# Memsets of the first batch's value tiles, written ahead of the loads into the same tiles

## The chip, the cores and the metric

The kernel runs on one core of a Trainium2 chip. The metric is the device time of one execution in microseconds (us), taken as the median of several executions. The profile is that of one execution; its times count from the start of its span.

## The reference

The reference is an attention with a relative position bias, followed by a feed-forward layer with a "snake" activation. Cut to what is computed:

```python
# q, k, v: [8 batches, 8 heads, 576 rows, 64]; bias_table: [32 buckets, 8 heads]
scores = (1 / sqrt(64)) * q @ k.transpose(0, 1, 3, 2)
bucket = ...            # of abs(row - column), 32 buckets
scores = scores + bias_table[bucket].transpose(2, 0, 1)[None]
attn = softmax(scores, axis=-1)
x = (attn @ v)  -> rows [8 * 576, 8 * 64]
h = x @ w_in                                   # [4608, 2048]
g = h + sin(alpha * h) ** 2 / (alpha + 1e-9)
out = g @ w_out                                # [4608, 512], float32
```

## The kernel before

The work is done batch by batch, eight times attention and then the feed-forward layer on blocks of 512 rows. In attention, keys and queries lie transposed (tiles `kT`, `qT`), one score tile of 128 keys by 512 queries for two heads is made by two matmuls, ScalarE (ACT) takes its exponential into `u`, VectorE (DVE) multiplies the stretch near the diagonal by a table of exponentiated biases (`m`, and its shifted copy `mh`), and TensorE (PE) multiplies with the values in `v`. The last 64 of the 576 keys go through tiles of their own, `kt` and `vh`. Each head has 65 columns in the value tiles: 64 of values and one column of ones, whose product is the sum of the softmax.

There are two tiles of each kind, for even and odd batches. Batch 0 is loaded straight from the inputs. Head pair 0 of its keys and queries arrives in `natx` through the queues of SP and ACT (L463), is cast by DVE (`cast0`, L498, and L542) and ACT (L543), is transposed by PE (L572) and copied to `kT` and `qT` by DVE (L561). Head pairs 1 to 3 arrive in `nat` through POOL's queue (L463) and are transposed by L578. The values come through POOL's queue too, four loads of 128 rows (L445, tile `v`) and two of the last 64 rows (L457, tile `vh`); a load writes columns 0 to 63 of each head, and a memset (L485) the column of ones. POOL then issues the loads of `w_in` (L468), of batch 1's keys and queries, of `w_out` (L472) and of batch 1's values.

Before any of this, PE runs matmuls on a tile of zeros (`zz`), and DVE clears `zz` (L528), `vh` and `v` (`clear_v`, L481 to L485), `kt` (`clear_k`, L477 and L478), makes `less_last` (a difference of unit vectors for the bias table) and clears the second pair of value tiles.

The order of the instructions is fixed when the program is built. The head of the program, which the diff touches, runs in the order in which its lines stand. Behind it a planner (`Plan`) orders the work of all engines by priorities and estimated times; each engine executes its own list in order. Which waits an instruction carries follows from the order of the source: whoever comes second into a tile waits for who came first. This holds for the tile as a whole here: the memset of the column of ones and the loads of the other 64 columns write different addresses, and still the later one waits for the earlier one. `STATIC` holds four loads that are issued in the head: keys and queries of head pair 1, and the first two of the value loads. The other two value loads and the two of `vh` are issued by the planner's first tasks on POOL.

```python
STATIC = ((1, (1, 0)), (1, (1, 1)), (0, (0,)), (0, (1,)))
LOADS = ((0, (2,)), (0, (3,)), (0, (4,)), (0, (5,)), (1, (2, 0)), ...
```

Of the kernel before, what the change touches and what calls it, by code (L numbers as in the profile page):

```python
# [303 lines left out]
def kernel(  # L304
# [11 lines left out]
    nc = tc.nc  # L316
# [44 lines left out]
    zz = sgl.tile([128, 512], F16, name="zz")  # L361
# [93 lines left out]
    def load_vt(t, z):  # L455
        vq = v[t].rearrange("(hp two) s d -> two s hp d", two=2)
        nc.gpsimd.dma_start(  # L457
            out=vhs[t % 2][64 * z : 64 * z + 64, :, VC * z : VC * z + D], in_=vq[z, 512:S]
        )
# [16 lines left out]
    def clear_k(eng, i):  # L476
        eng.memset(kts[i][0:64, :, 64:128], 0.0)  # L477
        eng.memset(kts[i][64:128, :, 0:64], 0.0)  # L478

    def clear_v(eng, i):  # L480
        eng.memset(vhs[i][0:64, :, VC : 2 * VC], 0.0)  # L481
        eng.memset(vhs[i][64:128, :, 0:VC], 0.0)
        eng.memset(vhs[i][0:64, :, D : D + 1], 1.0)
        eng.memset(vhs[i][64:128, :, VC + D : VC + D + 1], 1.0)
        eng.memset(vs[i][:, :, :, D : D + 1], 1.0)  # L485
# [34 lines left out]
    def load_v0(c):  # L520
        if c < 4:
            load_v16c(0, c)
        else:
            load_vt(0, c - 4)

    for t, f in STATIC:
        (load_kq1 if t else load_v0)(*f)
    nc.vector.memset(zz, 0.0)  # L528
    clear_v(nc.vector, 0)
    clear_k(nc.vector, 0)  # L530
    clear_k(nc.vector, 1)
    nc.vector.tensor_scalar(
# [773 lines left out]
```

## Time and profile before

| what | value |
|---|---|
| median of 3 executions | 381.05 us (380.95 to 381.33) |
| the profiled execution, its own time | 381.91 us |
| its span, first to last instruction | 380.2 us |
| mean granted clock of TensorE | 0.987 |
| PE busy | 365.0 us, 96% of the span |
| ACT busy | 313.5 us, 82% |
| DVE busy | 267.4 us, 70% |
| POOL busy | 87.8 us, 23% |

A row of the timeline gives the start of a group of instructions, its busy time, the engine, the line, the operation, the tile written and the tile read, the count (x), and in brackets the idle time of the engine just before and what ended it. PEld is the loading of weights into TensorE. A row of the windows gives each engine's busy time in a stretch, with the count in brackets, then the granted clock (PEclk, 1.00 is full), the time that the DMA engines were busy in it, and GB/s. A row of the DMA issues ends with the median time from the issue to the landing of the data.

### The profile page before, as it was taken

What the parts mean: (1) busy time and instruction counts of PE and PEld (TensorE: products, weight loads), DVE (VectorE), ACT (ScalarE), POOL (GpSimd) and SP (SyncE); (2) the same over time, 40 slices, a digit from 0 to 9 for tenths busy, and PEclk for the clock granted to TensorE, in tenths of its full rate; (3) what the DMA queues carried; (4) which work ended last, traced back from release to release, by engine and by line L of the source; (5) the groups of instructions that cost most, each with busy time, mean ns of one, the idle gap of its engine ahead of it and who ended that gap; (6) DMA issues with size and microseconds to landing.
All of it is one profiled execution on the core that took longest, in us unless ns stands there. A gap on an engine that the chain in (4) does not pass through costs nothing.

```text
span 380.2 us, 9067 instructions
## 1 busy us (share of the span) xinstructions
PE 365.0 (96%) x3662; PEld 199.9 (53%) x3662; DVE 267.4 (70%) x585; ACT 313.5 (82%) x428; POOL 87.8 (23%) x111
## 2 busy tenths in 40 slices
PE   3688999999999999999999999999999999999996
PEld 1556445554456445686464445544567455444443
DVE  0799698759775886678777967696769676879200
ACT  1199799979998999889997999798979997989211
POOL 4584250009100270019000900082006000000000
PEclk9599999999999999999999999999999999999999
DMA  9599999269921899289925992499339322000122
GB/s 135 39 164 209 203 154 118 57 126 94 157 78 47 132 133 156 58 133 109 165 73 93 132 162 65 106 117 157 88 73 154 55 66 53 9 1 30 57 81 83
DMA packets 147993, 39.16 MB, mean 103 GB/s; under 512 B 136416, under 2 KB 142960, under 8 KB 147952
## 3 DMA queue, kind: packets, MB, share of 16 engines
q0 software_dynamic: 99664, 18.06, 59.6%
q1 hardware_dynamic: 47920, 20.11, 22.7%
q8 instruction: 28, 0.46, 0.5%
q10 hardware_dynamic: 368, 0.43, 0.4%
q14 instruction: 13, 0.11, 0.1%
HBM read 36.84 MB, written 16.52 MB: 140 GB/s over the span
## 4 chain that ended last, share of the span: by engine, by line
PE 87%; DMA 6%; DVE 3%; POOL 2%; issue 1%; ACT 0%; ACTq 0%; DVEq 0%; POOLq 0%
PE pb L488 86%; DMA w_out<-in_moe_w_out_dram 5%; DMA v<-in_v_dram 1%; POOL nat L463 1%; PE pb L578 1%; PE pb L1089 0%; DVE kT L561 0%; DVE g L1147 0%; PE pb L572 0%; DVE kt L601 0%; POOL v L445 0%; POOL kt L601 0%; DVE tmp_a L713 0%; DVE m L561 0%; ACT s L1133 0%
## 5 line engine op out<-in xcount | busy, mean ns | idle before, releaser
L771 ACT ACTIVATE u<-pb 128x1024 f16<-128x1024 f32 (+1 forms) x146 | 136.9, 1019 | 12.1 <-PE pb L488 11.3
L488 PE MATMUL pb<-w_out,g 128*128 128x512 f16 (+2 forms) x592 | 138.9, 374 | 0.7 <-DMA w_out<-in_moe_w_out_dram 0.7
L488 PE MATMUL pb<-xT,w_in 128*128 128x512 f16 (+4 forms) x704 | 127.3, 340 | 0.0
L1133 ACT ACTIVATE s<-pb,alphaT 128x512 f16<-128x512 f32 x144 | 92.5, 693 | 15.0 <-PE pb L488 14.5
L1147 DVE SCALAR_TENSOR_TENSOR g<-sq,inv_a,pb 128x512 f16<-128x512 f16 x144 | 100.7, 743 | 4.9 <-ACT sq L1140 3.1
L488 PEld LDWEIGHTS <-w_in 128*128 128x128 f16 x704 | 64.8, 98 | 58.9 <-issue 1.0
L488 PEld LDWEIGHTS <-g 128*128 128x128 f16 x592 | 53.4, 98 | 60.9 <-issue 6.7
L803 DVE TENSOR_TENSOR u<-u,m 128x768 f16<-128x768 f16 (+1 forms) x128 | 62.0, 492 | 32.0 <-ACT u L771 30.1
L488 PEld LDWEIGHTS <-u 128*128 128x128 f16 x1152 | 44.1, 97 | 9.7 <-issue 3.5
L1140 ACT ACTIVATE sq<-s 128x512 f16<-128x512 f16 x73 | 45.7, 640 | 2.0 <-DVE g L1147 1.2
L441 POOL COPY kt<-kT 64x256 f16<-64x256 f16 x12 | 5.0, 421 | 174.4 <-DMA kT<-staged_k 174.1
L488 PE MATMUL pb<-v,u 128*128 128x65 f16 x1024 | 44.3, 193 | 0.1
L488 PE MATMUL pb<-qT,kT 64*128 64x64 f16 (+1 forms) x512 | 42.1, 287 | 1.6 <-ACT u L771 1.4
L1142 DVE TENSOR_TENSOR sq<-s 128x512 f16<-128x512 f16 x71 | 29.6, 421 | 16.5 <-ACT s L1133 16.0
L445 POOL DMA_DIRECT2D v<-in_v_dram x32 | 28.4, 898 | 12.9 <-DVE v L485 4.2
L1018 DVE TENSOR_TENSOR xn<-pb,rd 128x256 f16<-128x256 f32 (+2 forms) x59 | 28.5, 483 | 2.0
L488 PE MATMUL pb<-vh,u 128*128 128x130 f16 x128 | 28.2, 220 | 0.0
L488 PEld LDWEIGHTS <-kT 64*128 64x128 f16 x512 | 16.5, 94 | 21.7 <-issue 14.4
L561 DVE COPY outs<-pb 128x512 f32<-128x512 f32 x29 | 19.9, 686 | 2.1 <-PE pb L488 1.9
L559 ACT ACTIVATE outs<-pb 128x512 f32<-128x512 f32 (+2 forms) x8 | 4.4, 544 | 19.8 <-PE pb L488 19.8
L1211 ACT ACT_TABLE_LOAD x15 | 19.2, 1283 | 0.3
L1017 DVE RECIPROCAL rd<-pb 128x4 f32<-128x4 f32 (+2 forms) x59 | 10.9, 185 | 11.4 <-PE pb L488 11.4
(72 smaller groups left out, 190.7 us busy)
## 6 DMA issues: line engine op xcount, KB each, us to landing
out_dram<-outs SPq DMA_DIRECT2D x35, 256.0 KB, 2.3
v<-in_v_dram POOLq DMA_DIRECT2D x32, 128.0 KB, 4.6
staged_k<-in_k_dram POOLq DMA_DIRECT2D x6, 576.0 KB, 9.0
staged_q<-in_q_dram POOLq DMA_DIRECT2D x6, 576.0 KB, 12.1
w_out<-in_moe_w_out_dram POOLq DMA_DIRECT2D x4, 512.0 KB, 21.4
w_in<-in_moe_w_in_dram POOLq DMA_DIRECT2D x2, 512.0 KB, 8.7
w_in<-in_moe_w_in_dram POOLq DMA_DIRECT2D x1, 1024.0 KB, 13.8
xT<-xn SPq DMA_TRANSPOSE x47, 2.6
```

What stands on the lines that cost most here:

```text
L445: nc.gpsimd.dma_start(out=vs[t % 2][:, c, :, 0:D], in_=vp[128 * c : 128 * c + 128],)
L488: nc.tensor.matmul(out=out, lhsT=lhsT, rhs=rhs, start=start, stop=stop)
L561: k_of(e).tensor_copy(out=o, in_=i)
L771: nc.scalar.activation(out=o, in_=x, func=AF.Exp, scale=0.125)
L803: nc.vector.tensor_tensor(out=io, in0=io, in1=m2[:, 2 * p : 2 * p + 2, x0 : x0 + hi - lo], op=ALU.mult)
L1017: nc.vector.reciprocal(out=r, in_=x[:, :, :, D])
L1018: nc.vector.tensor_tensor(out=xn[:, 0:n].rearrange("p c (z d) -> p c z d", z=2), in0=x[:, :, :, 0:D], in1=r.unsqueeze(3).to_broadcast([128 ...
L1133: nc.scalar.activation(out=s16.v, in_=h.v, func=AF.Sin, scale=alphaT[:, f : f + 1])
L1140: nc.scalar.activation(out=sq.v, in_=s16.v, func=AF.Square)
L1142: k_of(e).tensor_tensor(out=sq.v, in0=s16.v, in1=s16.v, op=ALU.mult)
L1147: nc.vector.scalar_tensor_tensor(out=gcell[b].v[:, f, :], in0=sq.v, scalar=inv_a[:, f : f + 1], in1=h.v, op0=ALU.mult, op1=ALU.add,)
L1211: nc.scalar.preload_act_table_set(name)
```

## The change

The two lines that clear `zz` and the value tiles of even batches move from behind the four loads of `STATIC` to ahead of them. Nothing else changes.

```diff
+    nc.vector.memset(zz, 0.0)
+    clear_v(nc.vector, 0)
     for t, f in STATIC:
         (load_kq1 if t else load_v0)(*f)
-    nc.vector.memset(zz, 0.0)
-    clear_v(nc.vector, 0)
     clear_k(nc.vector, 0)
     clear_k(nc.vector, 1)
```

The memsets are on DVE and the loads on POOL, so neither engine's list changes its order; what changes is who waits. On DVE, at the very start of the program, the difference is this (`v_72` and `vh_74` are the value tiles of even batches, `kt_70` the key tile; DMASW4 and DMASW3 count the landings of the first two value loads; minus is before, plus is the change):

```order
-L528 MEMSET zz 128x256
+L526 MEMSET zz 128x256
 L481 MEMSET vh_74 64x4x65
 L482 MEMSET vh_74 64x4x65
 L483 MEMSET vh_74 64x4
 L484 MEMSET vh_74 64x4
-L485 MEMSET v_72 128x32 [waits DMASW4_49,DMASW3_49]
+L485 MEMSET v_72 128x32
 L477 MEMSET kt_70 64x4x32
 L478 MEMSET kt_70 64x4x32
```

The memset of the column of ones loses its wait for two loads; the rows around it are as they were. On POOL, in the head of the program behind the loads of head pair 1, the difference is this (`nat_96` holds head pairs 1 to 3; the wait is for a memset on DVE):

```order
 L463 DMA nat_96<-in_k_dram 96x2x384
 L463 DMA nat_96<-in_q_dram 96x2x384
-L445 DMA v_72<-in_v_dram 128x8x64 x2
 L445 DMA v_72<-in_v_dram 128x8x64 [waits DVE_49]
-L445 DMA v_72<-in_v_dram 128x8x64
+L445 DMA v_72<-in_v_dram 128x8x64 x3
 L457 DMA vh_74<-in_v_dram 64x4x64
 L457 DMA vh_74<-in_v_dram 64x4x64 [waits DMASW0_49]
```

The wait for DVE moves from the third value load to the first. PE, ACT and SP have the same rows and the same waits as before.

## The prediction

> **What bounds the kernel now.** I read the chain of work that ended last first, since it tells which stretch of the span could give anything back.
>
> ```profile
> 4.13 0.89 POOL v L445
> 5.02 4.44 DMA v<-in_v_dram
> ...
> 11.81 0.59 DVE natx L498
> ...
> 26.07 18.92 DMA w_out<-in_moe_w_out_dram
> ...
> 45.03 3.83 PE pb L488 x17
> ```
>
> The chain enters the value load in the first 10 us, comes out on DVE, and goes by POOL's queue into the landing of `w_out`; from 45 us on it is on PE almost without a break until 377. So a shift of the first 45 us passes through to the end unchanged, as long as the later stretches hang on nothing but PE's own list. The page's row of PE, busy tenths in 40 slices of 9.5 us, says the same:
>
> ```profile
> PE   3688999999999999999999999999999999999996
> ```
>
> From the fifth slice to the last but one it stands at 9; only the first four have anything to give.
>
> Next the timeline of DVE in the head.
>
> ```profile
> 2.01 0.06 DVE L484 MEMSET vh<- 64x4 f16 x1
> 9.71 0.09 DVE L485 MEMSET v<- 128x32 f16 x1 [7.63 <-DMA v<-in_v_dram]
> 10.60 0.38 DVE L532 TENSOR_SCALAR less_last<-idf_sb 32x128 f32<-32x128 f32 x1
> 11.81 0.58 DVE L498 CAST natx<-natx 96x768 f16<-96x768 f32 x1
> 12.30 0.39 DVE L542 CAST natx<-natx 96x384 f16<-96x384 f32 x1
> 13.14 0.76 DVE L561 COPY kT<-pb 128x576 f16<-128x576 f16 x1 [0.45 <-PE pb L572]
> 14.57 0.76 DVE L561 COPY qT<-pb 128x576 f16<-128x576 f16 x1 [0.19 <-PE pb L572]
> 18.18 1.22 DVE L561 CAST m<-pb 128x1024 f16<-128x1024 f32 x1 [0.31 <-PE pb L488]
> ```
>
> DVE stands still for 7.63 us ahead of one memset of 0.09 us, and everything of batch 0 is queued behind it: the cast of the first keys starts at 11.81.
>
> **The wait that goes.** Without it L485 follows L484 (its end is 2.07, and some 0.05 passes between neighbours) at 2.12 instead of 9.71, so DVE's list behind it is 7.59 us earlier, if nothing else is late. `less_last` would come at 3.01; its input is made by POOL in the row at 2.66 below and is ready at 2.86. The cast L498 would come at 11.81 - 7.59 = 4.22. What is late next are its data.
>
> ```profile
> natx<-in_k_dram ACTq DMA_DIRECT2D x1, 144.0 KB, 3.4
> ...
> 0.80 0.43 ACTq L463 DMA_DIRECT2D natx<-in_k_dram  x1
> 2.66 0.20 POOL L509 CAST idf_sb<-id_sb 32x32 f32<-32x32 f16 x1
> 5.19 0.52 ACT L543 ACTIVATE natx<-natx 96x384 f16<-96x384 f32 x1 [1.69 <-DMA natx<-in_q_dram]
> ```
>
> The keys of pair 0 land at 0.80 + 3.4 = 4.2, so L498 keeps about its 7.55. The queries land at 5.19, where ACT's row shows who waited for them; L542 can't start before, so it gains 12.30 - 5.19 = 7.1, and a new wait of about 0.4 us stands ahead of it. The copy to `kT` then starts at 5.6 (L542's end), a gain of 7.5. **First term: 7.5 us.**
>
> **The clock.** The second effect is on PE.
>
> ```profile
> 1.26 3.70 PE L488 MATMUL pb<-zz 128*128 128x512 f16 x12 [1.26 <-DVE zz L528]
> 12.44 0.66 PE L572 MATMUL pb<-id_sb,natx 96*128 96x96 f16 x6 [7.48 <-DVE natx L498]
> 15.21 0.69 PE L578 MATMUL pb<-id_sb,nat 96*64 96x96 f16 x12
> 17.00 0.61 PE L488 MATMUL pb<-qT,kT 64*128 64x512 f16 x2
> 19.61 0.39 PE L488 MATMUL pb<-qT,kT 64*128 64x512 f16 x2
> 21.83 0.45 PE L578 MATMUL pb<-id_sb,nat 96*64 96x96 f16 x12
> ...
> 8.75:9.00 0.25, 0.00 (x0) 0.00 (x0) 0.00 (x0) 0.00 (x0) 0.00 (x0) 0.96 0.10 6
> 9.00:9.50 0.50, 0.00 (x0) 0.00 (x0) 0.00 (x0) 0.00 (x0) 0.00 (x0) 0.50 0.00 0
> 19.00:19.25 0.25, 0.25 (x2) 0.00 (x0) 0.25 (x1) 0.25 (x1) 0.11 (x1) 0.56 0.85 92
> ```
>
> PE ends its first matmuls at 4.96 and sits idle until 12.44; the granted clock falls to 0.50 near 8.97, four microseconds into the gap, and comes back near 19.2. In between the same two score matmuls take 0.61 instead of 0.39, and twelve transposes 0.69 instead of 0.45. With the wait gone PE has its next transposes at 4.22 + 0.59 + 0.05 = 4.9, right behind its first matmuls, and the idle stretch that cost the clock isn't there. I take the clock as staying at 1.00. What that is worth on the path is not PE's halved time but DVE's idle time behind PE: 0.45, 0.19 and 0.31 us in the rows above, and 0.29, 0.34 and 0.40 between them, 2.0 us together. Bounds are 0 (the clock falls all the same) and 2.0 less the 0.45 that the new wait of L542 has taken, about 1.5. The transposes shrink by a third (0.69 to 0.45), which in DVE's idle time is about 0.25 us at each of the three later copies, and some 0.45 of the 0.6 at the bias table's small matmuls: I take 1.2. DVE and ACT then run ahead by 7.5 + 1.2 = 8.7 at 18 us, and ACT is dense from there to 36.9, so PE would ask for `w_out` 8.7 earlier. **Second term: 1.2 us, on DVE, ACT and PE.**
>
> The Trainium skill (page "TensorE: Matmul & The Clock Gate", part 1, on the clock gate) states that the clock halves after an idle window of about 3.4 us and returns after about 3.4 us of sustained work. The fall here after 4.0 us of idle agrees; the return after 6.8 us of nearly full work does not. By that rule the second term would stand in full, since no gap of 3.4 us is left.
>
> **POOL and the loads.** The chain goes by `w_out`, so POOL's list decides what can be kept.
>
> ```profile
> 4.12 1.80 POOL L445 DMA_DIRECT2D v<-in_v_dram  x2
> 10.09 1.76 POOL L445 DMA_DIRECT2D v<-in_v_dram  x2 [4.16 <-DVE v L485]
> 11.81 1.34 POOL L457 DMA_DIRECT2D vh<-in_v_dram  x2
> 16.77 0.51 POOL L601 COPY kt<-kT 64x64 f16<-64x64 f16 x2 [3.61 <-DVE kT L561]
> 17.22 0.65 POOL L463 DMA_DIRECT2D nat<-in_k_dram  x1
> 19.69 0.83 POOL L648 COPY mh<-m 64x768 f16<-64x768 f16 x1 [0.58 <-ACT m L559]
> 21.08 2.26 POOL L468 DMA_DIRECT2D w_in<-in_moe_w_in_dram  x3
> ```
>
> The added wait of the first value load is for a memset that is over by about 2.2, and POOL gets there at 4.12: it costs nothing, and the cover is 1.9 us. The third value load needn't wait any more (4.16 us), so POOL issues all six in one go: 4.12 + 1.80 + 1.76 + 1.34 = 9.02. The copy L601 waits for DVE's second `kT`, which ends at about 8.5 with the clock kept, so POOL goes on at once: 0.45 for the copy, then three loads of `nat` (17.22 to 19.11, 1.9 us) to 11.4. ACT's part of `m` is done by then (before: 0.58 us of waiting), so `mh` starts at 11.4 instead of 19.69, 8.3 earlier, and `w_in` at about 12.8, 8.2 earlier. `w_out` is three issues and one copy later on the same list.
>
> The DMA engines must follow. They are drained at 8.75 now, and the last two value loads and `vh` then move at leisure:
>
> ```profile
> 12.00:14.00 2.00, 1.56 (x13) 1.34 (x14) 1.45 (x4) 0.02 (x1) 1.16 (x2) 0.50 1.53 98
> 14.00:16.00 2.00, 2.00 (x43) 1.85 (x42) 1.26 (x5) 0.16 (x1) 0.00 (x0) 0.50 0.95 60
> 35.00:40.00 5.00, 4.98 (x59) 3.10 (x58) 2.87 (x10) 3.96 (x7) 1.40 (x2) 1.00 1.30 201
> ```
>
> That is 1.53 + 0.95, with the edges 2.6 us of engine time; put right behind the first two loads it lasts to about 11.4, before `w_in` starts. `w_in`, batch 1's keys and queries and `w_out` then stream at some 200 GB/s as now (last row), so the landing of `w_out` moves by the 8.2 of its issue, less perhaps 0.1 for the tail of the value loads. **What is kept: 8.1 us.** PE, 8.7 early, finds `w_out` only 8.1 early, and its wait there grows:
>
> ```profile
> 45.03 0.38 PE L488 MATMUL pb<-w_out,g 128*128 128x512 f16 x1 [0.74 <-DMA w_out<-in_moe_w_out_dram]
> ```
>
> from 0.74 to about 1.3 us. Bounds from both sides: 7.5 if the clock brings nothing, 9.0 if the loads keep up fully and the 0.74 is partly given back.
>
> **The sum.** The profiled execution took 381.91 (span 380.2 and 1.71 around it), 0.86 above the median. 381.91 - 8.1 = 373.8 for such an execution, and 0.86 less for the median: **372.9 us**.
>
> **Rivals.**
>
> *The clock falls all the same.* For it: between 12.44 and 19.2 PE was busy nearly throughout and the clock stayed low, so transposes and small matmuls may not count as full work. Against: the fall needed four idle microseconds. All of the head then moves by the first term only: 381.05 - 7.5 = 373.5.
>
> *DVE's work holds up POOL.* DVE is now busy between 2.1 and 9, where POOL issues eight loads that it issued beside an idle DVE. If each DVE instruction that reads and writes SBUF shut POOL out for its time (`less_last` 0.38, L498 0.58, L542 0.39, copies of `kt` 0.35, together 1.7), `w_out` would keep 8.1 - 1.7 = 6.4: 374.6. Against it: the value loads at 10.09, beside memsets and `less_last`, took 1.76, and those at 4.12, beside an idle DVE, 1.80; and `vh` at 11.81, beside both casts, took 0.67 each. The Trainium skill (page "SBUF — State Buffer", section "Who interferes with whom") states this as an exclusive lock of a port pair that VectorE's fast modes and GpSimd share, with the loser fully blocked. The issues just named show nothing of that size.
>
> *More than forecast.* If the stream of loads catches up, PE keeps 8.7 to 9.0: 372.2.
>
> *The wait is only moved.* Were DVE's memset late, POOL's first value load would wait for it; that needs a delay of over 1.9 us, and would leave 381 as it is.
>
> *Slower: POOL's queue waits for a value load.* Each load on POOL's queue waits for the one eight places ahead, so the first load of `w_in` waits for the third value load. That one is now issued at 5.9 into a busy queue, no longer at 10.1 into an empty one. The landing times of the value loads range widely:
>
> ```profile
> DMA to landing us min/median/max: 3.7/9.7/22.2
> ```
>
> If it took the longest, 22.2 us, it would land at 28.1, `w_in` would start 7.0 later than the 21.08 of now, and with it `w_out`: 388. It is slower than before from a landing at about 21, 15 us after the issue. Against it: that maximum comes from the stretch in which `w_in` and `w_out` fill the queue, and the second of the two early loads landed 4.44 us after its issue at 5.02 (the chain's row), with the engines as full as they will be for the third.
>
> **How the numbers follow.** Forecast, 372.9 (372.3 to 373.2): 0.52. Clock falls, 373.5: 0.24. POOL held up, 374.6: 0.09. More, 372.2: 0.11. Wait only moved, 381: 0.01. Slower: 0.02; the last 0.01 is for a gain of less than 6 us by other causes. The range reaches from the better case with 0.4 us for the uncertain sizes to the held-up POOL: 371.8 to 374.7. What a measurement of this kernel can tell from no change is about 0.2%, 0.8 us: faster 0.97, same 0.01, slower 0.02.
>
> **What the profile afterwards would show.** L485 at about 2.1 with no idle time; L498 at 4.2 to 4.3; L542 at 5.2 behind a short wait for the queries; the granted clock at 1.00 throughout (or a fall between 8 and 12, in which case the second term goes); all six value loads issued by 9.1; `w_in` at about 12.8; PE's first matmul with `w_out` at about 36.9, behind a wait of 1 to 1.5 us; and the rest of the timeline the same but for that shift. The prediction is wrong if the wait of PE for `w_out` is far longer, or if the stretch after it no longer runs at PE's pace.

## The result, and the profile after

| | before | changed |
|---|---|---|
| median, 4 executions each | 381.19 us (380.95 to 381.43) | 375.25 us (374.40 to 375.51) |
| ratio | 1 | 0.984 (0.9823 to 0.9858) |
| the profiled execution | 381.91 us | 375.07 us |
| its span | 380.2 us | 373.4 us |

The change makes the kernel 5.9 us faster. 8.1 were forecast, and the range ended at 374.7.

The page of the changed kernel, busy tenths and granted clock in slices of 9.3 us:

```profile
PE   8799999999999999999999999999999999999996
PEclk9789999999999999999999999999999999999999
```

Of the four slices that had something to give, the first goes from 3 to 8 and the last two reach 9, but the second only goes from 6 to 7. The clock, forecast at full, dips in the second and third.

The timeline of DVE in the changed kernel (start, busy time, engine, line, operation):

```profile
2.23 0.09 DVE L485 MEMSET v<- 128x32 f16 x1 [0.16 <-issue]
4.34 0.58 DVE L498 CAST natx<-natx 96x768 f16<-96x768 f32 x1
5.18 0.37 DVE L542 CAST natx<-natx 96x384 f16<-96x384 f32 x1 [0.26 <-DMA natx<-in_q_dram]
9.17 1.23 DVE L561 CAST m<-pb 128x1024 f16<-128x1024 f32 x1
```

The wait of 7.63 us is gone, a new one of 0.26 stands ahead of L542, and the cast to `m` comes at 9.17 instead of 18.18, 9.0 earlier. The head of the program did what the first two terms said.

The timeline of PE in the changed kernel:

```profile
12.50 0.39 PE L488 MATMUL pb<-qT,kT 64*128 64x512 f16 x2 [0.37 <-ACT u L771]
14.27 0.69 PE L578 MATMUL pb<-id_sb,nat 96*64 96x96 f16 x12 [1.38 <-DMA nat<-in_k_dram]
17.02 0.61 PE L488 MATMUL pb<-qT,kT 64*128 64x512 f16 x2
38.26 0.38 PE L488 MATMUL pb<-w_out,g 128*128 128x512 f16 x1 [0.46 <-DMA w_out<-in_moe_w_out_dram]
```

At 12.89 PE has nothing left: the keys of head pair 2 have not landed, and it waits 1.38 us for them. Then the slow durations are back, 0.69 for twelve transposes and 0.61 for two score matmuls. The first matmul with `w_out` starts at 38.26; 36.9 was forecast. Three windows of the same kernel show the clock around that wait (columns: the stretch, its length, PE, PEld, DVE, ACT, POOL, granted clock, mean share of the DMA engines, GB/s; the share is no time, as the text ahead of the prediction calls it, and can pass 1: before, 12 to 13 us shows 1.82, 13 to 14 shows 1.24, and the window over both 1.53):

```profile
13.00:14.00 1.00, 0.00 (x0) 0.00 (x0) 0.69 (x3) 0.95 (x1) 0.85 (x2) 1.00 0.99 115
14.00:20.00 6.00, 5.73 (x62) 2.62 (x62) 4.35 (x8) 4.27 (x5) 5.56 (x9) 0.52 1.04 142
20.00:38.00 18.00, 16.91 (x211) 10.68 (x210) 14.23 (x41) 16.34 (x26) 6.49 (x9) 0.97 1.23 206
```

From 14 to 20 us the clock is at half, PE is nearly full, and DVE and ACT stand still for over a quarter of the time. The lead of 9.0 us that the head had won shrinks here. The chain of work that ended last, in the changed kernel:

```profile
4.14 3.88 POOL v L445 x4
...
9.74 4.48 DMA nat<-in_k_dram
14.27 0.71 PE pb L578 x12
15.00 0.77 DVE kT L561
...
16.69 1.49 POOL nat L463 x2
18.19 20.03 DMA w_out<-in_moe_w_out_dram
38.26 3.83 PE pb L488 x17
```

The chain leaves POOL for the keys of pair 2, which take 4.48 us to land behind the four value loads. Then it goes by PE, DVE and POOL into `w_out`, which takes 20.03 us from issue to landing; before, it took 18.92.

Behind this point nothing changed. From PE's first matmul with `w_out` to the end of the span there were 380.2 - 45.03 = 335.2 us before and 373.4 - 38.26 = 335.1 after. So the question is what sets that one start. Two things can: the landing of `w_out`, and PE's own arrival (the start less the wait in its row). Before, they were 44.99 and 44.29; in the changed kernel 38.22 and 37.80. **Both moved by less than forecast: the landing by 6.8 instead of 8.1, PE's arrival by 6.5 instead of 8.7.**

### The profile page after: what moved, and what is told of

The parts are those of the page before. It is cut to its first block, busy times and chain, and to the rows that moved or that the text cites. A ratio compares the mean times of both kernels' runs of the same rounds, so it can differ in the third digit from the quotient of the medians.

```text
span 373.4 us, 9066 instructions
## 1 busy us (share of the span) xinstructions
PE 364.9 (98%) x3662; PEld 198.9 (53%) x3662; DVE 267.3 (72%) x585; ACT 313.5 (84%) x428; POOL 87.7 (23%) x111
## 4 chain that ended last, share of the span: by engine, by line
PE 87%; DMA 7%; POOL 3%; DVE 1%; issue 0%; ACT 0%; ACTq 0%; POOLq 0%
PE pb L488 86%; DMA w_out<-in_moe_w_out_dram 5%; DMA nat<-in_k_dram 1%; POOL v L445 1%; POOL nat L463 1%; PE pb L578 0%; DVE kT L561 0%; PE pb L1089 0%; DVE g L1147 0%; POOL kt L601 0%; POOL vh L457 0%; DVE kt L601 0%; ACT s L1133 0%; DVE qT L561 0%; POOL tabN L503 0%
## 5 line engine op out<-in xcount | busy, mean ns | idle before, releaser
L1133 ACT ACTIVATE s<-pb,alphaT 128x512 f16<-128x512 f32 x144 | 92.5, 693 | 14.7 <-PE pb L488 14.2
## 6 DMA issues: line engine op xcount, KB each, us to landing
w_in<-in_moe_w_in_dram POOLq DMA_DIRECT2D x1, 1024.0 KB, 14.2
```

The costliest lines, as they stand in the source:

```text
L1133: nc.scalar.activation(out=s16.v, in_=h.v, func=AF.Sin, scale=alphaT[:, f : f + 1])
```

## The experiments

The theories were these. The landing: only the late `w_out` cost the rest. The keys and the clock: the keys of pair 2 come late behind the value loads, PE runs dry, the clock falls, and PE's own arrival is late as well. DMA capacity: with the head packed tighter, the DMA engines have no room left, and whatever is added to them delays `w_out`.

**One memset alone (ones_only).** From the kernel before, only the memset of the column of ones goes ahead of the loads; `zz` and the other memsets stay behind them.

```diff
...
+    nc.vector.memset(vs[0][:, :, :, D : D + 1], 1.0)
     for t, f in STATIC:
         (load_kq1 if t else load_v0)(*f)
     nc.vector.memset(zz, 0.0)
-    clear_v(nc.vector, 0)
+    clear_v(nc.vector, 0, ones=False)
```

> Of the moved memsets only that of the column of ones (0.09 us) stands ahead of the four loads; zz and the four memsets of vh stay behind them. Theory: the one wait of that memset is the whole change, so this runs as the changed kernel does, about 375.2 us, and DVE's idle time of 7.63 us is gone. Rival: that the memsets of zz and vh matter too (they now come 0.1 us later, and a load into vh gets a wait for them): then the time lies between 375.2 and 381.2.

374.57 us (373.81 to 375.19), ratio 0.9814 (0.9794 to 0.9835), beside 0.984 (0.9823 to 0.9858) of the change. The intervals overlap: the wait of this one memset accounts for the whole change, and the position of the others does nothing that was measured.

**Keys ahead of values (nat_first).** The changed kernel, with the loads of POOL's planned tasks in another order: the four of keys and queries of pairs 2 and 3 go out ahead of the last two of `v` and the two of `vh`. The places in the lists of all engines stay.

```diff
-        for t, f in LOADS:
-            if t:
-                pool("n%d%d" % f, 0.63, lambda f=f: load_kq1(*f), 1.05)
+        for (t, f), (t_, f_) in zip(LOADS, LOADS[4:] + LOADS[:4]):
+            go = lambda t_=t_, f_=f_: (load_kq1 if t_ else load_v0)(*f_)
...
```

> The changed kernel, with POOL's four loads of head pairs 2 and 3 issued ahead of the last two value loads and the two of vh; every other engine's list is the same. Theory A (two limits at once: the keys of pair 2 land late behind the value loads, which starves PE and ACT at 13 to 15 us; and the DMA engines, never empty from 2 us on, let w_out land only 6.8 us earlier than before): keys of pair 2 land at about 10 instead of 14.2, PE's gap of 1.38 us and ACT's of 1.59 go, PE asks for w_out 1 to 2 us earlier than in the changed kernel and waits that much longer, and the time falls by 0.5 at most: 374.7 to 375.2. Rival B (the fall of the clock at 15 us, caused by that gap, is what costs): no fall, w_out too is earlier, and the time falls by 1.5: 373.7. Rival C (POOL is held up by DVE): nothing moves, 375.2.

372.87 us (372.49 to 373.48), ratio 0.9772 (0.9755 to 0.9789): over 2 us below the changed kernel, and below all three expectations, of which the nearest was 373.7. In its timeline of PE:

```profile
9.53 0.61 PE L488 MATMUL pb<-qT,kT 64*128 64x512 f16 x2
14.17 0.39 PE L488 MATMUL pb<-qT,kT 64*128 64x512 f16 x2
14.49 0.45 PE L578 MATMUL pb<-id_sb,nat 96*64 96x96 f16 x12
36.74 0.38 PE L488 MATMUL pb<-w_out,g 128*128 128x512 f16 x1
```

The transposes of pair 2 follow the score matmuls with no wait, the short durations stay from there on, and PE comes to `w_out` at 36.74 on its own; the bracket of a wait is missing. `w_out` also landed earlier, at 18.80 (issue) + 17.4 = 36.2, though it was issued 0.6 later than in the changed kernel. That holds although the clock was low at the start: 0.61 us at 9.53, where the changed kernel took 0.39 at 8.24. So this run mends both, the keys and the landing, and doesn't tell them apart.

**`w_out` earlier (wout_first).** The changed kernel, with the first quarter of `w_out` issued ahead of batch 1's keys and queries, so that its landing is out of the way.

```diff
-                pool("kq%d" % kq, 0.8, lambda kq=kq: load_nat2(kq), 3.1)
+                pool("kq%d" % kq, 0.8, (lambda: load_w_out16(0)) if kq == 0
+                     else lambda: load_nat2(0), 3.1)
...
-            wq.append(("wo%d" % f, 0.76, lambda f=f: load_w_out16(f), 2.65))
+            wq.append(("wo%d" % f, 0.76, lambda f=f: load_w_out16(f) if f else load_nat2(1), 2.65))
```

> The changed kernel, with the first quarter of w_out issued ahead of batch 1's keys and queries. Theory A: w_out lands some 4 us earlier and PE's wait of 0.46 us for it goes, but PE itself is only 6.5 us earlier than before, so only the 0.46 is gained: about 374.8. Rival (the landing of w_out is the only limit): the time falls by 1.5 us or more, 373.7.

373.31 us (372.65 to 374.14), ratio 0.9781 (0.9756 to 0.9806). It was run again beside the changed kernel:

> The changed kernel with the first quarter of w_out ahead of batch 1's keys and queries, once more, beside the changed kernel on one chip. Theory D: 1.5 to 2 us below the changed kernel, 373.3; PE comes to the first matmul with w_out without a wait, between 35.9 (clock kept at full) and 37.3 (clock fallen near 15 us).

373.87 us (372.98 to 374.69), ratio 0.9798 (0.9773 to 0.9822). Two profiles of this one kernel, from the two sets, were taken of executions that differ. The timeline of PE in the first:

```profile
13.95 0.45 PE L578 MATMUL pb<-id_sb,nat 96*64 96x96 f16 x12 [0.68 <-DMA nat<-in_k_dram]
35.88 0.38 PE L488 MATMUL pb<-w_out,g 128*128 128x512 f16 x1
48.16 0.39 PE L488 MATMUL pb<-qT,kT 64*128 64x64 f16 x15 [0.54 <-DVE g L1147]
```

and in the second:

```profile
14.13 0.45 PE L578 MATMUL pb<-id_sb,nat 96*64 96x96 f16 x12 [1.13 <-DMA nat<-in_k_dram]
16.56 0.69 PE L578 MATMUL pb<-id_sb,nat 96*64 96x96 f16 x12
37.43 0.38 PE L488 MATMUL pb<-w_out,g 128*128 128x512 f16 x1
```

and two windows of the second:

```profile
15.00:16.00 1.00, 0.81 (x16) 0.53 (x15) 1.00 (x3) 1.00 (x2) 0.79 (x3) 0.89 0.98 135
22.00:23.00 1.00, 1.00 (x15) 0.80 (x13) 0.18 (x1) 0.94 (x3) 0.07 (x1) 0.70 1.14 216
```

In neither does PE wait for `w_out`. Where the keys cost 0.68 us of waiting the clock stayed up and PE arrived at 35.88; where they cost 1.13 the clock fell between 15 and 16, came back between 22 and 23, and PE arrived at 37.43, 1.55 later. The eight executions fall apart in the same way: the three whose mean granted clock was 0.991 took 374.14 to 374.69, the five at 0.995 to 1.00 took 372.65 to 373.63. This shows the second limit by itself: with the landing out of the way, late keys and the fall of the clock cost 1.35 us between the means of the two groups. In the two profiles 0.45 of the 1.55 us is the longer wait for the keys; that the rest is the clock's doing fits the longer durations, but the groups don't show it apart. The last row of the first profile shows a price of the edit: batch 1's keys come later, and the rest of the span is 371.9 - 35.88 = 336.0 us instead of 335.1.

**Both together (both).** The edits of nat_first and wout_first in one kernel.

> Both orders together. Theory A: both limits are gone, PE reaches its first matmul with w_out some 8.3 us earlier than before without a wait, and the time falls by about 1.8 us against the changed kernel, more than the two runs alone add up to: about 373.4. Rival B or the rival that w_out alone limits: no better than the better of the two single orders.

372.76 us (372.41 to 373.30), ratio 0.9769 (0.9752 to 0.9786), the same as nat_first alone. PE starts with `w_out` at 36.28; the quarter had landed 6 us before. Once the keys come first, an earlier `w_out` brings nothing more that can be told.

**The changed kernel again.**

> The changed kernel once more, for a second profile on the chip of the other runs of this set. Theory D (the landing of w_out is what bounds the changed kernel, and the DMA engines, never empty from 2 us on, set it): PE's first matmul with w_out starts within 0.1 us of that landing, at 37.3 to 38.7, and the span is that start plus 335.1 us, whatever the clock did in the head. Rival (PE's own chain, late by the fall of the clock and the late keys): PE arrives after w_out has landed. Time 374.4 to 375.5.

374.77 us (374.30 to 375.07), ratio 0.9828 (0.9813 to 0.9843). The timeline of PE in this execution:

```profile
13.94 0.45 PE L578 MATMUL pb<-id_sb,nat 96*64 96x96 f16 x12 [0.65 <-DMA nat<-in_k_dram]
37.91 0.38 PE L488 MATMUL pb<-w_out,g 128*128 128x512 f16 x1 [2.06 <-DMA w_out<-in_moe_w_out_dram]
```

Here the keys cost 0.65 us and the clock stayed at 1.00. PE arrived at 37.91 - 2.06 = 35.85, which is 8.44 earlier than before (8.7 were forecast), and it then stood still for 2.06 us: `w_out`, issued at 17.61, took 20.26 us. So in this execution, with the clock kept, the landing alone set the time of the changed kernel.

**The gap filled (wout_hold).** wout_first, with 14 more matmuls on `zz` ahead of the transposes of pair 2, to keep PE busy while the keys land.

```diff
-            c.v = bank(b).bitcast(F16)
+            c.v = bank(b).bitcast(F16)
+            for _ in range(14 * ((t, p, kq) == (0, 2, 0))):
+                full(bank(b)[:, 0:192], zz[:, 0:128], zz[:, 0:192], True, True)
```

> The kernel wout_first, with 14 more matmuls on the tile of zeros (192 columns, 1.2 us at full clock) ahead of the transposes of head pair 2's keys, where PE waits for their landing. If the fall of the clock near 15 us comes from that gap and costs: no fall, PE at the first matmul with w_out at about 35.9, and 0.5 to 1 us below wout_first, 372.5. If the clock is of no account: no difference, 373.3, or 0.3 above it where the extra matmuls last beyond the landing.

375.22 us at the median (372.91, 374.96, 375.48, 375.52), ratio 0.9828 (0.9795 to 0.986). The profile is of the 372.91: PE has no gap ahead of the keys, the clock stays up, and `w_out` starts at 35.89. The other three executions are over 2 us slower at a mean clock of 0.999 to 1.00, and no trace shows what they lost. This run is inconclusive, and it shows that a clock that stays up is not enough for the short time.

**`w_out` earlier in the kernel before (before_wout).** The edit of wout_first on the kernel before.

> The kernel before (with its wait of 7.63 us on DVE), with the first quarter of w_out ahead of batch 1's keys and queries. Theory D: there PE's own chain and the landing of w_out were 0.74 us apart, so no more than that is gained: 380.6 to 381.2, against 1.5 to 2 us in the changed kernel. Rival (that order is worth as much in either kernel): 379.6.

381.37 us, ratio 0.9999 (0.9986 to 1.0011). The first quarter landed at 38.6, 5.5 us ahead of its use, PE began with it at 44.08 without waiting, and the time is the same. In the kernel before, the wait of 0.74 us for `w_out` was not what the time hung on.

**More bytes in the head (extra_changed, extra_before, extra_both).** Four loads of 128 KB of a constant on SP's queue, behind a memset of DVE at 4.5 us, into columns of `w_out`'s tile that the true load writes over later.

```diff
-    clear_v(nc.vector, 1)
+    clear_v(nc.vector, 1)
+    nc.vector.memset(w_out16[:, 12:16, 0:1], 0.0)
+    for f in range(12, 16):
+        nc.sync.dma_start(out=w_out16[:, f, :], in_=phi_h.ap())
```

> The changed kernel with 512 KB more on the DMA engines in the head: four loads of 128 KB on SP's queue, behind DVE's clears (at about 4.5 us), into a part of w_out that is overwritten later. Theory D (the DMA engines are never empty from 2 us to the landing of w_out, which bounds the kernel): w_out lands later by the time of these bytes, 1.7 us at the 300 GB/s of the fastest stretch to 2.5 us at the 205 GB/s of the stream, and the kernel is that much slower than the changed one: 376.5 to 377.3. Rival (the issue by POOL sets the landing, not the engines): at most 0.5 us, 375.3.

> The same 512 KB in the kernel before, where they come at about 12 us, behind DVE's wait. Theory D: the DMA engines stand empty there for some 3 us from 15.1 on, so the bytes cost little: 381.2 to 381.9. Rival (the bytes cost their time wherever they are): 383 to 383.8.

> The same 512 KB in the kernel with both orders turned (loads of head pairs 2 and 3, and the first quarter of w_out, issued earlier), where w_out landed at 30.1 and PE came to it at 36.28. Theory D: 6 us of slack take the bytes, and the keys have slack too: 372.8 to 373.5. Rival (the bytes cost their time wherever they are): 374.5 to 375.3.

On the changed kernel 375.73 us (374.67 to 376.76), ratio 0.9855 (0.9832 to 0.9878), 0.5 to 1 us above the changed kernel (374.77 and 375.25), which the intervals don't separate, and less than the theory of DMA capacity expected. On the kernel before it is free: 381.73, ratio 1.0007 (0.9993 to 1.002). On both together 373.78 (373.47 to 373.88), ratio 0.9801 (0.9785 to 0.9818), about 1 us more than without the bytes and between the two expectations. That microsecond was lost behind the head: PE starts with `w_out` at 36.30, as it did without the bytes (36.28), and the rest of the span is 372.2 - 36.30 = 335.9 us instead of 335.0. What was lost in the changed kernel was not lost where the theory puts it either. Its chain of work, at the keys of pair 2:

```profile
9.76 5.70 DMA nat<-in_k_dram
```

and its timeline of PE:

```profile
15.50 0.45 PE L578 MATMUL pb<-id_sb,nat 96*64 96x96 f16 x12 [1.10 <-DMA nat<-in_k_dram]
17.93 0.69 PE L578 MATMUL pb<-id_sb,nat 96*64 96x96 f16 x12
38.81 0.38 PE L488 MATMUL pb<-w_out,g 128*128 128x512 f16 x1
```

The keys took 5.70 us instead of 4.48, the clock fell, and PE came to `w_out` at 38.81 without waiting: the bytes delayed the keys, not `w_out`. `w_out`, behind 512 KB more, landed earlier than in the changed kernel: 19.17 + 16.8 = 36.0 instead of 38.2. So the number of bytes ahead of it does not explain its 20 us, and this theory falls as far as one profile can tell.

**Both kernels again (changed_look3, changed_look4, before_look2, before_look3).** One profiled execution each, nothing edited.

> The changed kernel, one more look. If the longer flight of w_out (19.5 to 20.3 us in three profiles, against 18.92 in the one of before) belongs to the changed kernel, because its DMA engines carry a backlog when w_in starts: 19.5 or more again, and w_in's last part 14.2 to 14.4 after its issue. If it is a variation of the stream from execution to execution, as between wout_first (w_in's last part after 14.3) and wout_hold (12.3), which issue the same loads: it can be 17 to 18 here.

> The changed kernel, a further look, as for changed_look3: by the theory of the backlog w_out's flight is 19.5 us or more, by that of a variation between executions anywhere from 17 to 20.3.

> The kernel before, one more look. Backlog theory: w_out's flight below 19, here as in the first profile (18.9). Variation: from 17 to 20. In either case PE's own arrival at its first matmul with w_out is 43.6 to 44.3, and where w_out lands earlier than that, the wait of 0.74 us is gone and the span is some 0.7 us shorter, 379.5.

> The kernel before, a further look, as for before_look2: by the theory of the backlog w_out's flight is below 19 us, by that of a variation between executions from 17 to 20, with the wait of 0.74 us there or not.

The changed kernel took 374.69 and 374.48 us. The start of PE's first matmul with `w_out`, first in changed_look3, then in changed_look4:

```profile
37.88 0.38 PE L488 MATMUL pb<-w_out,g 128*128 128x512 f16 x1 [0.90 <-DMA w_out<-in_moe_w_out_dram]
```

```profile
37.74 0.38 PE L488 MATMUL pb<-w_out,g 128*128 128x512 f16 x1
```

In both the keys cost over 1.6 us (1.74 and 1.64) and the clock fell near 15. In one the landing was last, in the other PE itself, and the times agree within 0.2 us: the two limits lie side by side. The kernel before took 381.43 and 381.49 us, with this row in before_look2 (in before_look3 it reads 44.77):

```profile
44.73 0.38 PE L488 MATMUL pb<-w_out,g 128*128 128x512 f16 x1
```

There is no wait for `w_out` in either. The 0.74 us in the prediction's profile belonged to that one execution. The flight of `w_out`, from issue to landing, was 18.0 and 17.0 us in these two; with the first profile's 18.92 all three of before lie under all five of the table below (19.4 to 20.3), as the theory of the backlog expected (one, at 19.4, is a tenth under its bound). But nat_first (17.4) and extra_changed (16.8), which load at least as many bytes, lie under them too.

All profiles of the changed kernel, and of ones_only, which acts as it does, side by side:

| profile | PE's wait for keys | clock | PE's arrival | `w_out`: issue, flight, landing |
|---|---|---|---|---|
| changed | 1.38 us | fell | 37.80 | 18.19 + 20.03 = 38.22 |
| changed_again | 0.65 | stayed | 35.85 | 17.61 + 20.26 = 37.87 |
| changed_look3 | 1.74 | fell | 36.98 | 18.22 + 19.62 = 37.84 |
| changed_look4 | 1.64 | fell | 37.74 | 18.10 + 19.4 = 37.5 |
| ones_only | 0.84 | fell | 37.33 or just before | 17.77 + 19.52 = 37.29 |

The wait alone doesn't order the arrivals: changed_look3 waited longest and arrived first of the four whose clock fell. There the half clock lasted 3.4 us (14.74 to 18.15), in the other three 6.8 us (in the first row from 14.22 to 21.04).

## Why the prediction was wrong, by its own steps

**Right.** The wait that goes: L485 at 2.23, DVE's list 7.1 to 7.7 us earlier up to the first copy to `kT`, L542 behind a short wait for the queries. By ones_only this wait is all that the change removes. The added wait on POOL costs nothing, as forecast. POOL's issues came within 0.4 us of theirs: `w_in` at 13.07 (12.8 forecast), `w_out` at 17.61 to 18.22 (17.87). The stretch from the first matmul with `w_out` on is unchanged, at 335.1 us. Of the rivals, two showed in small. DVE's work holds up POOL: the four value loads took 3.90 us to issue, where 1.80 + 1.76 = 3.56 were forecast, and the difference sits in the first of them, 1.27 us instead of 0.92, which DVE's cast L498 (0.58 us) falls into. In wout_first that load took 0.92, and there the cast took 1.05. So one of the two held up the other in each of these executions. And POOL's queue waits for a value load: the second load of `w_in` waited 0.26 us for one in changed_look3.

**The step that failed: "What is kept: 8.1 us".** It is a term that was mis-sized. The landing of `w_out` moved by 6.8 us in the profiled pair. Of the missing 1.3, some 0.3 are the later issue (18.19 against 17.87), the rest the time from issue to landing, which I carried over from before at 18.9 plus 0.1 and which was 19.4 to 20.3 in the five profiles of the table. The reason given there was that the value loads last "to about 11.4, before `w_in` starts", so that `w_in` streams at 200 GB/s from its start. Its "1.53 + 0.95" added two shares of the DMA engines as if they were microseconds. Each stood for a window of 2 us, so the sum is 5.0 us, and from 8.75 it reaches to 13.7, past the start of `w_in`. In the changed kernel the last value load and the two of `vh` landed at 13.7 to 14.0. The step also left out the four loads of keys and queries behind them, issued from 9.74 on, of which the first landed at 14.2. The six microseconds from 0.9 us after the issue of `w_in` moved 142 GB/s (in the window of 14 to 20 above). Before, the same stretch shows:

```profile
22.00:28.00 6.00, 5.10 (x91) 3.20 (x88) 5.97 (x14) 6.00 (x8) 5.53 (x9) 1.00 1.11 172
```

30 GB/s less for 6 us are 180 KB, 0.9 us at 206 GB/s, about the size of the longer flight (1.1). So a backlog ahead of `w_in` has the right size, but that it is what slows the stream is not shown. The pace in that stretch doesn't order the other executions (changed_again moved 164 GB/s and its flight was the longest), and extra_changed, with 512 KB more and a flight of 16.8, speaks against the number of bytes.

**The second step that failed: "I take the clock as staying at 1.00".** The mechanism was right where it was looked for: the gap between the first matmuls and the first transposes is closed, and with the clock kept PE arrives 8.44 us earlier (changed_again), beside a forecast of 8.7. What was missing is a term for the next landing, that of pair 2's keys. They are issued behind the value loads at 9.74, and PE, 9 us early, is now there ahead of them. It waited 0.65 to 1.74 us for them, and in four of five profiles the clock fell after that; PE then arrived at 36.98 to 37.80 instead of 35.85. My rival "the clock falls all the same" had the fall right, though not its time or its occasion: it spoke of transposes and small matmuls that may not count as full work, with a fall between 8 and 12 us, and not of a wait for later keys at 13 to 15. Its price was the first term alone, a move of 7.5 us; PE's arrival in the profiled pair moved by 6.5. That the order of these loads counts was shown by nat_first, which has neither the wait nor the fall and gains over 2 us; it also shortens the flight of `w_out`, and which of the two brings more there stays open.

For the clock I had leaned on the Trainium skill (page "TensorE: Matmul & The Clock Gate", part 1): a fall needs an idle window of about 3.4 us. The longest single gap ahead of these falls was 1.74 us, the shortest 0.84. The rule and the measurement differ, and the measurement decides. My own reason, "the fall needed four idle microseconds", was drawn from a single fall, and showed only that four are enough.

**The offset, 0.86 us.** The sum was 373.8 for the profiled execution, which took 375.07. From this I took 0.86, the distance of the profiled execution of before to its median. That distance held for the one execution: the profiled execution of the changed kernel lies 0.18 under its median. So of the 2.35 us between 372.9 and 375.25, 1.27 are the sum and 1.04 the offset (with rounding). The two further profiles of before, 381.43 and 381.49 us, begin with `w_out` 0.3 us earlier than the execution that I read.

**Why neither failure alone accounts for the time.** In the changed kernel the timed executions with a recorded mean clock of 0.999 or 1.00 (374.30 to 375.51) and those at 0.990 or 0.991 (374.40 to 375.42) are equally long: in the one profile where the clock stays, PE waits for `w_out` instead. With the landing removed (wout_first), the clock shows up as 372.65 to 373.63 against 374.14 to 374.69.

**The better version.** nat_first and both together, 372.87 and 372.76 us, are 8.5 and 8.6 us below the kernel before on the same chip (381.40) and about 2 below the changed kernel.

## What to carry to other kernels

Where a long wait at the head goes, list every transfer that the earlier work will ask for, in the order of its queue, the small ones too, and see for each whether it moves as far as its consumer; here the loads of 144 KB that stood behind value loads nobody needed yet became the next thing waited for, and putting them first brought another 2 us. Before two shares of a busy column are added, multiply each by its window. A memset and a load that share a tile are worth ordering by hand, since the memset of a column stood 7.6 us behind a load of other columns. And before a distance between a profiled execution and the median enters a sum, profile several executions: a wait of 0.74 us in one was absent in the next two.

## What the runs showed of the hardware that was not expected

The clock fell after gaps of PE between 0.84 and 1.74 us, in all six profiles of the changed kernel, ones_only, wout_first and extra_changed in which the wait for the keys was that long, and in neither of the two in which it was 0.65 or 0.68. Eight cases show an order and no more. Between the end of the gap and the fall lay up to 1.8 us of transposes and short matmuls; in the changed kernel's first profile the fall came at the end of the gap itself.

The granted clock in the record can read 1.00 where it was not. In nat_first it reads 1.00 throughout, yet at 9.53 two score matmuls took 0.61 us, as they did before at 0.50. There the durations tell the clock more surely than the record does.

The time from issue to landing of the same load differs between executions of one kernel by 1 to 2 us: `w_out` took 18.92, 18.0 and 17.0 us in three profiles of the kernel before.
